# A planned kernel's first stores of weight sums and its transposing transfers: new dependences, new planned costs, a new order

## The chip, the cores and the metric

The kernel runs on one core of one Trainium2 chip. The metric is the device time of one execution in microseconds (us). The time before is 708.41 us, the median of 3 runs (707.8 to 711.64).

## The reference, cut to what matters

```python
xn = layernorm(x)                                  # x: 2048 x 1024, bf16
# A: sliding dilated attention, 32 heads of 32, 8 keys per query at distances 0, 2, ..., 14
q, k, v = split(xn @ wqkv)                         # wqkv: 1024 x 3072
attn = softmax(mask(q . k[pos - 2 w]) * 32 ** -0.5)
s = (sum_w attn[w] * v[pos - 2 w]) @ wo            # wo: 1024 x 1024
# B: gated product
g = silu((silu(xn @ w1) * (xn @ w3)) @ w2)         # w1, w3: 1024 x 3584, w2: 3584 x 1024
out = x + s * g
```

## The kernel before

The 2048 rows are four chunks (c) of 512 rows, two chunks to a block (b). A block goes through the q, k and v products, the gate and up products (14 steps of two 128-column tiles, numbered by f tile), the down product and the output product with wo; the attention of a chunk runs on VectorE (DVE) beside the products. Nearly every product of a block is done as a fast matrix product of the Strassen-Winograd kind: 2 by 2 parts (two chunks by two halves of the contraction), seven products in place of eight, with sums of the weights (S, in fp16, four per weight matrix, two to a 1 MB row buffer) and sums of the transposed rows (xs). In block 0 the weight sums are made on DVE and stored in DRAM by GpSimd (POOL) for block 1 to load.

**The start.** The rows of chunk 0 and chunk 1 (x0, x1) are loaded and normalized by tiles of 128 rows. Chunk 0 is transposed on TensorE (PE) by way of PSUM. Of chunk 1, row tiles 0 to 2 are transposed by six transposing transfers on SyncE (SP), one for each tile and half of the columns: turn1_0_0, turn1_0_1, turn1_1_0, turn1_2_0, turn1_1_1, turn1_2_1 (chunk, tile, half; made in turn_half, line 680 of the profile); tile 3 is transposed on PE (tp1_3, two halves). While they run, PE does the products of chunk 0 with the first and second half of the q and k weights (fq0 to fq3, fk0 to fk3). DVE then makes, in an order that is written out by hand (plan.chains): the weight sums qs0f, qs1f; the row sums xs0, xs0b; qs3f; xs1, xs2; qs2f; xs3. The sum qs3f overwrites the row buffer of x1, which the transfers read. qs0f and qs1f lie in the row buffer S[0], qs3f and qs2f in S[1]; qkv_sums stores each with one 1 MB store on POOL (put_sq0_0, put_sq0_1). After the chain come, in the planner's order, the sums of the k weights and the two additions of the first pair of q products, qc12 and qc22; the products that follow on PE write the banks that qc22 reads. SP goes on, behind the transposing transfers, with loads of w2 parts (w2q), whose sums DVE makes in gaps.

**What sets the order.** Nothing is issued in the order in which the program text stands. Each operation is an entry of a Plan: its engine, a name, a function that emits the instruction, lists of the cells that it reads and writes, its planned time on the engine (occ), and for a transfer its bytes. Plan.depend makes planned dependences from the lists; Plan.limits works due times back from the TensorE order; Plan.simulate walks through it with these costs and takes, on each engine, the ready entry with the earliest due time (ties by the place in the program):

```python
for i in sorted((i for i in ready[e] if ops[i].ready <= T), key=lambda i: (ops[i].limit, i)):
```

A transfer is planned to occupy one shared pipe for its bytes over its rate, and to land 1.3 us later. Plan.replay repeats the walk once for each entry of ORDER: an entry's first part adds to the due times of operations, given by their number in the plan, and its second part moves a TensorE operation from one place in TensorE's order to another. The order of the last walk is what is emitted, engine by engine. The instruction itself is made by the entry's function, as in the helper for transfers, which does not hand on the lists:

```python
plan.op(eng, name, lambda: e.dma_start(out=o(), in_=a()), rd, wr, occ, 0.0, nbytes=kb * 1024, late=late)
```

The semaphores on the chip are set by the framework from the tiles that the emitted instructions name. Some lists hold cells that stand for no tile: the four transposing transfers of a later chunk (turn2, turn3, in ln_turn, line 688; turn2 on ScalarE's (ACT) queue, turn3 on SP's) read a cell "pr" that a product marks.

**Block 0's down product**, about 245 to 330 us: chunks 2 and 3 are loaded into row buffers, normalized on ACT (mean2, var2, mean3, var3 and so on), and transposed by turn2 and turn3; the halves of w2 and of its sums are loaded into row buffers that come free (rhs_load). One of these, number 1350 in the plan, is the first half of w2 for the products de0_0 to de0_3 (rhs_load("w", 1, 1)), and number 1351 is the second; 1343 to 1345 are turn3_1 to turn3_3.

Of the kernel before, what the change touches and what calls it, by code (L numbers as in the profile page):

```python
# [10 lines left out]
FP16 = mybir.dt.float16  # L11
# [3 lines left out]
PE, DVE, ACT, POOL, SP = range(5)  # L15
# [27 lines left out]
class Plan:  # L43
# [209 lines left out]
    def replay(self):  # L253

        pes = self.pes = [o.idx for o in self.ops if o.eng == PE]
        self.simulate()
        for late, swaps in [((), ())] * 2 + list(ORDER):
            for i, d in late:
# [15 lines left out]
            o.emit()  # L274


ORDER = (((), ((29, 26), (29, 26), (29, 26), (29, 26), )),
((), ((27, 26), (27, 26), )),
((), ((27, 26), (27, 26), )),
(((647, -0.7), ), ()),  # L280
(((684, 1.9), ), ()),
(((684, 1.8), ), ()),
((), ((243, 242), )),
(((1076, 0.5), (684, 1.1), ), ((244, 242), )),
(((684, 3.3), (684, 7.4), ), ((245, 243), )),
(((1004, 1.1), (1175, 3.5), (1077, 0.7), ), ()),
(((695, -0.4), ), ()),
(((1074, 3.8), (1074, 5.3), (1077, 1.4), ), ((248, 247), )),
(((1077, 0.3), ), ((251, 250), )),
(((695, -0.3), (718, -0.3), (1077, 0.7), (690, 0.6), ), ()),  # L290
((), ((27, 26), (27, 26), )),
(((1012, -0.8), ), ((370, 368), )),
(((1010, 0.4), (1010, 0.5), (1006, 0.4), ), ()),
(((1006, -0.2), (999, 0.3), ), ((371, 369), )),
(((1010, 1.6), ), ((370, 369), )),
(((1010, 0.9), (1010, 0.7), ), ((368, 370), (371, 370), )),
((), ((371, 370), )),
(((1012, 1.5), ), ()),
(((1225, 0.3), (1217, 1.6), (1112, 9.6), ), ()),
(((1222, 0.9), (1223, -0.4), ), ()),  # L300
(((1192, 1), (1177, 0.7), (1180, 1.6), (1179, -1), ), ()),
(((1193, 10.9), (1193, 10.3), ), ()),
((), ((375, 377), )),
(((1012, 0.6), ), ((370, 369), )),
(((1220, -0.3), ), ()),
(((1175, 10.8), (1006, 0.2), (1175, 3.6), ), ((368, 371), )),
(((1276, 0.4), ), ()),
(((1126, 7.6), ), ((405, 403), )),
(((1305, 4.1), (1350, -4.2), (1311, 3.1), (1277, 4.6), (1174, 0.3), ), ((423, 417), )),
(((1347, 1.8), ), ((422, 417), )),  # L310
(((1174, 0.4), (997, 8.3), (1344, 1), (1304, 0.4), ), ()),
((), ((427, 426), )),
(((1347, 1.4), ), ()),
((), ((419, 417), )),
(((1174, 0.8), ), ()),
(((1176, 0.6), (1012, -0.6), ), ()),
(((1173, 0.3), (1004, 2), (1173, 0.4), (1174, 0.5), ), ()),
(((1012, -0.4), (1012, -0.2), (1012, -0.5), (1173, 0.8), ), ()),
(((1175, 0.5), ), ((377, 376), )),
(((1012, -0.4), (1012, -0.2), ), ((369, 368), )),  # L320
(((1472, 6.6), (1345, 0.5), (1343, 0.3), ), ()),
(((1387, -0.6), (1343, 0.3), ), ((435, 434), )),
((), ((27, 26), (27, 26), )),
((), ((25, 26), (25, 26), )),
((), ((458, 455), )),
((), ((456, 455), (456, 455), )),
((), ((458, 456), )),
(((1513, 0.2), ), ()),
(((1513, 0.7), (1513, 0.5), ), ()),
(((1527, 0.5), (1525, 0.6), ), ((461, 460), )),  # L330
(((2454, 7.2), (2448, 1.4), (2262, 1.3), (2067, -1.6), (2452, 3.5), (2262, 2.7), (2326, 2.7), ), ((756, 761), (761, 758), )),
(((2060, 0.7), (2066, 3.4), (2067, -3), (2061, 3.1), ), ()),
(((2326, -4), ), ()),
(((2069, -2.2), (2065, 1.6), (2452, 4), (2281, 2.7), ), ((761, 759), (457, 455), )),
(((1946, -0.3), (2326, -0.4), (2011, 2.5), (2026, 4.2), ), ()),
(((2312, 0.5), (2312, 0.4), ), ()),
((), ((457, 455), (455, 453), (457, 455), )),
(((1729, 4.5), (1679, 1.1), (2323, 0.9), ), ((594, 592), )),
(((2326, -0.3), (2334, 0.5), ), ()),
(((2312, 0.8), (1875, 0.4), ), ()),  # L340
((), ((593, 596), (598, 596), )),
(((1755, 0.5), (1752, 11.9), (1743, 15.3), (1878, -0.3), (1862, 0.6), (1748, 4.1), ), ((597, 595), )),
(((2310, 0.5), (2312, 0.3), ), ((761, 760), )),
)
LAST = []

# [2 lines left out]
def kernel(  # L349
# [13 lines left out]
    S, D, F = 2048, 1024, 3584  # L363
# [38 lines left out]
    sq_dram = {t: dram.tile([2, P, 4096], FP16, name=f"sq{t}_dram") for t in RL}  # L402
# [24 lines left out]
    plan = Plan()  # L427
# [84 lines left out]
    def dma(eng, name, o, a, rd, wr, kb, late=0.0):  # L512
        e = {SP: nc.sync, POOL: nc.gpsimd, ACT: nc.scalar}[eng]
        occ = {SP: 0.45, POOL: 0.58, ACT: 0.42}[eng]
        for part, cost in COST:
            if name.startswith(part):
                kb = kb * cost
                break
        plan.op(eng, name, lambda: e.dma_start(out=o(), in_=a()), rd, wr, occ, 0.0, nbytes=kb * 1024, late=late)
# [22 lines left out]
    def r8v(s, dt=BF16):  # L542
        a = s.ap()
        return a.bitcast(dt) if dt != BF16 else a
# [20 lines left out]
    def xrow(xt, st):  # L565
        return xt.ap().rearrange("p (s d) -> p s d", s=NST)[:, st, :]
# [110 lines left out]
    def turn_half(c, st, xt, kh):  # L677

        half, cut = c % 2, slice(kh * CH, (kh + 1) * CH)
        plan.op(SP, f"turn{c}_{st}_{kh}", lambda: nc.sync.dma_start(  # L680
            out=xT[:, half, kh * KH:(kh + 1) * KH, st * P:(st + 1) * P], in_=xrow(xt, st)[:, cut], transpose=True),
            [(xt, st)], xt_cells(half, kh, st), 0.7, 0.0, nbytes=128 * 1024)

    def ln_turn(c, st, xt, cell):

# [1279 lines left out]
```

## Time and profile before

| | |
|---|---|
| median of 3 runs | 708.41 us (707.8 to 711.64) |
| the profiled execution | 709.42 us |
| its span, first to last instruction | 707.6 us |
| granted TensorE clock | 1.0 |
| TensorE busy | 699.7 us, 99% |
| VectorE busy | 674.8 us, 95% |
| ScalarE busy | 399.0 us, 56% |
| HBM read and written | 161 MB, 228 GB/s over the span |

Columns of the timeline: start and length in us, engine, line, operation, written and read tiles, shape, count, and in brackets the engine's idle time just before with what ended it. Engines with a q are their sequencers; a transfer's issue is there, its landing is not. Lines are those of helpers: 478 is a product, 487 an addition, subtraction or multiplication on DVE, 492 a copy on ACT, 519 a plain transfer, 680 and 688 transposing ones. Tiles have the program's names without numbers: r is a row buffer, so r<-r,r on DVE is a sum of weights; xT the transposed rows; mm a PSUM bank; k a buffer of f32 halves; qo the q values. TENSOR_TENSOR r<-r,r and qo<-mm,k of about 1.2 us start 1.14 us apart when nothing holds them. The chain of waits has start, length and what was on it; the waits have total, times and longest.

### The profile page before, as it was taken

How to read it: one execution, taken by the hardware profiler on the slowest of the kernel's cores; microseconds unless marked ns; L12 is line 12 of the kernel's file. 1: busy time of each engine (PE TensorE's matmuls, PEld its weight loads, DVE VectorE, ACT ScalarE, POOL GpSimd, SP SyncE). 2: the span in 40 equal slices, each digit the busy share in tenths (PEclk: the TensorE clock that was granted, in tenths of full speed). 3: DMA queues.
4: the chain of work that ended last, by engine and by line, in shares of the span. 5: the costliest groups of instructions: out<-in, count | busy, mean ns of one | idle time of the engine just before them, and what ended most of it. 6: DMA issues, size and time to landing. Idle time of an engine off the chain costs nothing.

```text
span 707.6 us, 9945 instructions
## 1 busy us (share of the span) xinstructions
PE 699.7 (99%) x3666; PEld 374.1 (53%) x3666; DVE 674.8 (95%) x827; ACT 399.0 (56%) x752; POOL 48.4 (7%) x93
## 2 busy tenths in 40 slices
PE   8999999999999999999999999999999999999997
PEld 5555555555555474744555554555555555656443
DVE  7898999999999999999979999999999999999956
ACT  7644465758575799612555355656766865222233
POOL 1010011112110010100010000000100010000000
PEclk9999999999999999999999999999999999999999
DMA  9999898964986679894896559973766575957502
GB/s 324 289 413 383 266 340 309 324 221 138 355 282 213 233 249 253 283 272 124 333 323 245 178 175 337 315 234 131 223 219 198 188 220 173 349 189 242 178 27 92
DMA packets 138239, 174.06 MB, mean 246 GB/s; under 512 B 16912, under 2 KB 112800, under 8 KB 131536
## 3 DMA queue, kind: packets, MB, share of 16 engines
q1 hardware_dynamic: 126128, 132.33, 58.6%
q0 software_dynamic: 7408, 39.61, 15.0%
q10 hardware_dynamic: 4656, 1.51, 1.1%
q8 instruction: 28, 0.46, 0.3%
q14 instruction: 19, 0.16, 0.1%
HBM read 117.31 MB, written 43.78 MB: 228 GB/s over the span
## 4 chain that ended last, share of the span: by engine, by line
PE 83%; DVE 9%; DMA 3%; issue 2%; ACT 1%; SPq 1%; DVEq 0%; POOL 0%; ACTq 0%
PE mm L478 73%; PE mm L1423 6%; PE mm L1152 4%; DVE r L487 2%; DVE a L487 2%; DMA s_dram<-r 1%; DVE qo L487 1%; DVE h_sb L487 1%; DMA r<-in_A_wqkv_dram 1%; DVE k L487 1%; DMA r<-in_A_x_dram 1%; DMA xT<-r 0%; DVE mm L487 0%; DVE small L583 0%; ACT k L492 0%
## 5 line engine op out<-in xcount | busy, mean ns | idle before, releaser
L478 PEld LDWEIGHTS <-r 128*128 128x128 f16 (+1 forms) x2068 | 219.4, 108 | 200.8 <-issue 1.9
L478 PE MATMUL mm<-xs,r 128*128 128x512 f16 x1280 | 300.1, 379 | 1.3 <-DVE qo L487 0.8
L478 PE MATMUL mm<-xT,r 128*128 128x512 bf16 (+2 forms) x788 | 178.8, 370 | 1.7 <-DMA r<-in_A_wqkv_dram 1.0
L492 ACT COPY k<-mm 128x512 f32<-128x512 f32 (+1 forms) x226 | 123.6, 558 | 75.9 <-PE mm L478 69.3
L478 PE MATMUL mm<-r,h_sb 128*128 128x512 f16 (+1 forms) x592 | 129.7, 379 | 0.0
L492 ACT COPY mm<-mm 128x512 f32<-128x512 f32 (+1 forms) x157 | 76.4, 489 | 93.6 <-PE mm L1152 33.0
L478 PEld LDWEIGHTS <-h_sb 128*128 128x128 f16 (+1 forms) x680 | 66.5, 98 | 78.8
L487 DVE TENSOR_TENSOR a<-a 128x2048 bf16<-128x2048 bf16 (+7 forms) x106 | 107.1, 1011 | 0.7
L487 DVE TENSOR_TENSOR h_sb<-mm,k 128x1024 bf16<-128x1024 f32 x48 | 58.1, 1217 | 7.0 <-PE mm L478 7.0
L487 DVE TENSOR_TENSOR a<-qo,kT 128x2048 bf16<-128x2048 bf16 x48 | 57.7, 1217 | 0.2
L1152 PE MATMUL mm<-xT,r 128*128 128x256 f16 (+1 forms) x364 | 56.9, 273 | 0.0
L487 DVE TENSOR_TENSOR h_sb<-h_sb 128x1024 f16<-128x1024 bf16 (+7 forms) x74 | 54.3, 746 | 0.0
L487 DVE TENSOR_TENSOR a<-E,vT 128x2048 bf16<-128x2048 bf16 x42 | 50.2, 1216 | 0.0
L1152 PEld LDWEIGHTS <-r 128*128 128x128 f16 (+1 forms) x364 | 35.6, 98 | 26.5
L487 DVE TENSOR_TENSOR r<-r,r 128x1024 f16<-128x1024 f16 (+7 forms) x56 | 42.8, 768 | 3.0 <-DMA xT<-r 1.5
L509 ACT ACTIVATE k<-k 128x512 bf16<-128x512 f32 x56 | 32.2, 622 | 22.9 <-DVE k L487 22.9
L487 DVE TENSOR_TENSOR k<-mm,k 128x1024 f32<-128x1024 f32 (+1 forms) x44 | 44.9, 1022 | 0.2
L509 ACT ACTIVATE h_sb<-mm 128x512 bf16<-128x512 f32 x60 | 36.3, 606 | 13.6 <-PE mm L478 12.3
L487 DVE TENSOR_TENSOR qo<-qo,a 128x2048 bf16<-128x2048 bf16 x32 | 38.9, 1216 | 0.0
L487 DVE TENSOR_TENSOR r<-r 128x1024 f16<-128x1024 bf16 (+4 forms) x71 | 35.9, 514 | 0.8 <-DMA r<-in_A_wqkv_dram 0.8
L487 DVE TENSOR_TENSOR h_sb<-h_sb,k 128x2048 bf16<-128x2048 bf16 x28 | 34.0, 1216 | 0.0
L492 ACT CAST k<-mm 128x512 bf16<-128x512 f32 x56 | 31.4, 605 | 0.5 <-PE mm L478 0.5
(131 smaller groups left out, 535.9 us busy)
## 6 DMA issues: line engine op xcount, KB each, us to landing
r<-in_B_w_dram SPq DMA_DIRECT2D x42, 512.0 KB, 6.2
s_dram<-r POOLq DMA_DIRECT2D x14, 1024.0 KB, 6.1
r<-s_dram SPq DMA_DIRECT2D x14, 1024.0 KB, 5.0
r<-t_dram SPq DMA_DIRECT2D x15, 896.0 KB, 7.3
r<-in_A_wqkv_dram SPq DMA_DIRECT2D x10, 1024.0 KB, 7.4
r<-in_B_w_dram SPq DMA_DIRECT2D x11, 896.0 KB, 5.8
h_sb<-in_B_w_dram SPq DMA_DIRECT2D x14, 512.0 KB, 8.6
t_dram<-h_sb POOLq DMA_DIRECT2D x7, 1024.0 KB, 7.8
```

What stands on the lines that cost most here:

```text
L478: nc.tensor.matmul(cut(ps.ap()), lhsT=lhs[k](), rhs=cut(rhs[k]()), start=(first and k == 0), stop=(last and k == n - 1), skip_group_check= ...
L487: plan.op(DVE, name, lambda: fn(out=o(), in0=a(), in1=b()), rd, wr, occ, 0.08, late=late)
L492: plan.op(ACT, name, lambda: nc.scalar.copy(out=o(), in_=a()), rd, wr, occ, 0.11)
L509: plan.op(ACT, name, lambda: nc.scalar.activation(out=o(), in_=a(), func=ACTF.Silu), rd, wr, occ, 0.11, table="silu")
L1152: nc.tensor.matmul(half(pa[i].ap, n)(), lhsT=A[0][k](), rhs=B[0][k](), start=first and k == 0, stop=k == 1, skip_group_check=True)
L1423: nc.tensor.matmul(half(bank.ap, n)(), lhsT=a[k](), rhs=c[k](), start=first and k == 0, stop=k == NQ - 1, skip_group_check=True)
```

## The change

Three things are done. First, in block 0 the two stores of the q weights' sums (t = 0, the only call with early > 0) list as read, besides their own cells, those that turn1_1_1 and turn1_2_1 write. Second, the planned costs are new: a transposing transfer of chunk 1 is planned as 1.35 us of SP in place of 0.7 and as 1.4 times its bytes, the general rate of transfers is 3.45e5 bytes per us in place of 3.25e5, and 3.7e5 is set between the chunk-1 transfers and the weight sums of q. Third, ORDER is replaced: 118 entries in place of 67.

```diff
-ORDER = (((), ((29, 26), (29, 26), (29, 26), (29, 26), )),
+ORDER = (((), ((39, 44), (44, 42), )),
+((), ((39, 44), (44, 42), )),
+((), ((27, 26), )),
...
-(((1305, 4.1), (1350, -4.2), (1311, 3.1), (1277, 4.6), (1174, 0.3), ), ((423, 417), )),
-(((1347, 1.8), ), ((422, 417), )),
-(((1174, 0.4), (997, 8.3), (1344, 1), (1304, 0.4), ), ()),
...
-(((1472, 6.6), (1345, 0.5), (1343, 0.3), ), ()),
-(((1387, -0.6), (1343, 0.3), ), ((435, 434), )),
...
+(((1065, 0.5), ), ((222, 228), (228, 226), )),
...
+(((1175, 0.4), ), ((368, 364), )),
...
+((), ((454, 452), (457, 456), (452, 451), )),
...
+(((2060, 2.6), (2448, 5.9), (2058, 2.7), (2323, 0.7), ), ((539, 538), )),
...
@@ turn_half
-            [(xt, st)], xt_cells(half, kh, st), 0.7, 0.0, nbytes=128 * 1024)
+            [(xt, st)], xt_cells(half, kh, st), 1.35, 0.0, nbytes=int(1.4 * 128 * 1024))
@@ qkv_sums
-                dma(POOL, f"put_sq{t}_{i}", lambda i=i: sq_dram[t][i], lambda i=i: r8v(S[i], FP16), c(2 * i) + c(2 * i + 1), [("sqd", t, i)], 1024)
+                dma(POOL, f"put_sq{t}_{i}", lambda i=i: sq_dram[t][i], lambda i=i: r8v(S[i], FP16),
+                    c(2 * i) + c(2 * i + 1) + (xt_cells(1, 1, 1) + xt_cells(1, 1, 2) if early else []), [("sqd", t, i)], 1024)
@@ the program's loop over the blocks
-    RATE = 3.25e5
+    RATE = 3.45e5
...
-            plan.rate = RATE
+            plan.rate = 3.7e5
             qkv_first("k", wk, lambda j: ln_tp(1, j, x1, (ACT, ACT)), turned=3)
             xn_sums()
+            plan.rate = RATE
             sq = qkv_sums(b, 0, wq, 30.0, ([("ln", 1, 3)], [], xs_cells(1)))
```

Carried out one after the other, the exchanges of the old ORDER and of the new one give these TensorE orders where they differ: at places 39 to 43 the old has tp1_3, fk0, fk1, fk2, fk3 and the new fk1, tp1_3, fk0, fk3, fk2; at 417 to 424 the old has the halves of de0 in the order 0a, 2a, 3a, 0b, 1a, 1b, 2b, 3b and the new 0a, 0b, 1a, 1b, 2a, 2b, 3a, 3b; and the new moves single products at 222 to 232, 364 to 376, 451 to 462, 538 to 543, 823, 829 and 854, and no longer moves those at 426, 434, 592 to 598 and 756 to 761.

More of the change, by code (lines that the diff above doesn't have):

```diff
@@ L274, in run @@
             o.emit()
-ORDER = (((), ((29, 26), (29, 26), (29, 26), (29, 26), )),
+ORDER = (((), ((39, 44), (44, 42), )),
+((), ((39, 44), (44, 42), )),
+((), ((27, 26), )),
+((), ((27, 26), )),
 ((), ((27, 26), (27, 26), )),
-((), ((27, 26), (27, 26), )),
[L280 to L287, printed above, removed]
@@ L288 @@
-(((1074, 3.8), (1074, 5.3), (1077, 1.4), ), ((248, 247), )),
-(((1077, 0.3), ), ((251, 250), )),
-(((695, -0.3), (718, -0.3), (1077, 0.7), (690, 0.6), ), ()),
-((), ((27, 26), (27, 26), )),
[L292 to L308, printed above, removed]
-(((1305, 4.1), (1350, -4.2), (1311, 3.1), (1277, 4.6), (1174, 0.3), ), ((423, 417), )),
-(((1347, 1.8), ), ((422, 417), )),
-(((1174, 0.4), (997, 8.3), (1344, 1), (1304, 0.4), ), ()),
@@ L312 @@
[L312 to L320, printed above, removed]
-(((1472, 6.6), (1345, 0.5), (1343, 0.3), ), ()),
-(((1387, -0.6), (1343, 0.3), ), ((435, 434), )),
-((), ((27, 26), (27, 26), )),
-((), ((25, 26), (25, 26), )),
@@ L325 @@
[L325 to L343, printed above, removed]
+((), ((27, 26), )),
+((), ((24, 26), (24, 26), (24, 26), )),
+((), ((27, 26), )),
+((), ((44, 42), (42, 44), )),
@@ new lines @@
+((), ((27, 26), )),
+((), ((29, 26), (29, 26), (29, 26), )),
+((), ((29, 26), )),
+((), ((27, 26), )),
+((), ((25, 26), (25, 26), )),
+((), ((25, 26), (25, 26), )),
+((), ((27, 26), )),
+((), ((27, 26), )),
+((), ((45, 44), (45, 44), )),
+((), ((27, 26), )),
+((), ((27, 26), )),
+((), ((27, 26), )),
+((), ((27, 26), (27, 26), )),
+((), ((27, 26), )),
+((), ((40, 44), (44, 41), )),
+((), ((45, 44), (45, 44), )),
+((), ((44, 42), (44, 42), (43, 44), )),
+(((1065, 0.5), ), ((222, 228), (228, 226), )),
@@ new lines @@
+(((1067, 1), (1066, 2.4), (646, 2.3), (1066, 2), (653, 3.8), (1067, 1.8), ), ((222, 227), )),
+((), ((225, 226), (226, 223), )),
+((), ((229, 228), )),
+((), ((232, 230), )),
+((), ((231, 230), )),
+((), ((45, 44), (45, 44), )),
+((), ((226, 229), )),
+(((646, -0.5), ), ()),
+(((657, 12.1), (654, 4.5), (647, 0.8), (657, 10), ), ((229, 228), )),
+((), ((44, 43), (44, 43), )),
+((), ((44, 41), (41, 44), )),
+((), ((43, 44), (44, 41), )),
+((), ((44, 42), (42, 44), )),
+(((1175, 0.4), ), ((368, 364), )),
@@ new lines @@
+((), ((27, 26), (27, 26), )),
+(((997, 0.3), ), ()),
+(((1173, 0.9), ), ()),
+(((997, 0.3), (1173, 5.1), ), ((376, 372), )),
+((), ((371, 372), )),
+((), ((376, 371), )),
+((), ((43, 44), (44, 42), )),
+((), ((372, 371), )),
+((), ((370, 371), (370, 371), )),
+((), ((372, 371), )),
+(((1222, 0.2), (1220, -0.4), (1225, 0.7), ), ((373, 371), )),
+(((1177, 0.5), ), ()),
+(((1192, 4.3), ), ()),
+(((1177, 1), (1193, 12.1), (1193, 13.4), (1179, 0.9), ), ()),
+(((1173, 3.9), (1179, 1.1), ), ()),
+(((1177, 0.8), ), ()),
@@ new lines @@
+(((1220, -0.7), ), ()),
+(((1177, 8.8), ), ((374, 377), (377, 372), )),
+(((1173, 11.8), (1223, -0.4), ), ()),
+(((1222, 0.6), ), ()),
+(((1126, 3.6), (1312, -2.7), ), ()),
+(((1202, 0.7), ), ()),
+(((1179, 5.8), (1202, 12.6), (1179, 2.2), (1194, 0.3), ), ()),
+(((1277, 0.9), (1299, -0.5), ), ((405, 403), )),
+(((1180, 0.3), ), ()),
+((), ((458, 455), (455, 452), )),
+(((1433, -0.5), ), ()),
+(((1161, 0.5), ), ()),
+((), ((454, 452), (457, 456), (452, 451), )),
+((), ((462, 459), )),
+(((1179, 0.3), (1195, 0.4), (1220, -0.2), ), ((458, 456), )),
@@ new lines @@
+(((1180, 0.1), (1180, 0.5), ), ()),
+(((1513, 0.6), ), ()),
+(((1513, 4.2), ), ()),
+(((1528, 0.5), ), ()),
+((), ((461, 460), )),
+(((1180, 0.2), ), ()),
+(((1220, -0.2), ), ()),
+(((1179, 0.4), ), ()),
+(((1220, -0.1), ), ()),
+(((1179, 0.4), (1180, 0.2), ), ()),
+(((1179, 0.2), ), ()),
+(((1179, 0.3), ), ()),
+(((1220, -0.2), ), ()),
+(((1180, 3.1), (1180, 5.7), (1228, 0.5), ), ()),
+(((1241, -0.8), (1180, -1.1), (1180, -1.3), ), ()),
+(((1228, 1), (1227, 1.4), (1220, 1.7), ), ()),
+(((1299, 1.4), (1299, 1.9), (1194, 4.7), (1305, 1.1), (1304, -1.1), (1194, 3.9), (1221, 1), (1304, -1.3), (1277, 1.4), (1183, 0.3), ), ((374, 377), )),
@@ new lines @@
+(((1256, -0.2), (1236, 0.7), ), ((377, 376), )),
+(((2365, 0.2), (1179, 0.2), ), ()),
+(((2458, 0.4), (2463, 0.5), ), ()),
+(((1173, 4), ), ((826, 824), )),
+(((1119, 0.5), (2498, 9.9), (1181, 0.4), ), ()),
+(((2507, -1), (1225, 12.4), ), ()),
+(((2480, 0.5), (2532, 0.4), ), ((824, 823), )),
+(((1239, 0.8), ), ((823, 828), )),
+(((1180, 0.2), (1256, -1.6), (1195, 0.2), (1181, 1.1), ), ()),
+(((2060, 2.6), (2448, 5.9), (2058, 2.7), (2323, 0.7), ), ((539, 538), )),
+(((2290, -0.2), ), ((827, 826), (543, 538), )),
@@ new lines @@
+(((2470, 0.7), ), ()),
+(((1180, 0.5), (1195, 0.3), (1195, 0.4), ), ()),
+(((2511, -0.6), (1220, -0.2), ), ((822, 826), )),
+(((2509, 0.7), ), ()),
+(((1220, -0.3), (1180, 0.5), ), ((823, 822), )),
+((), ((827, 825), )),
+(((1180, 0.6), (1220, -0.2), (1180, 0.5), (2516, 0.7), ), ()),
+(((2511, 1.1), (2511, 0.8), (1179, 0.3), (2476, 1.3), ), ()),
+(((2511, -0.6), (2525, 0.5), ), ((825, 824), )),
+(((2476, 1), (2507, -1.6), ), ()),
+(((1179, 0.3), (2498, 1.6), (2476, 0.4), ), ((830, 828), )),
+(((2476, 6.7), ), ((825, 824), )),
@@ L344 @@
+(((2511, -0.3), (1180, 0.7), (2498, 2.5), (1180, 0.2), ), ()),
+(((1180, 0.5), (2475, 3), ), ((855, 854), )),
+((), ((827, 825), (825, 822), )),
+(((1195, 1.9), (2692, 4.4), (2591, 0.4), (2589, 0.9), ), ()),
+(((2695, 3.6), ), ()),
+(((1195, 0.2), ), ((829, 826), )),
 )
```

## The prediction

> **What bounds the kernel now.** I read the page first, for who is busy; then TensorE's waits, for what is left to win; then the timeline of the first 38 us, where most of it lies; then the chain of waits through it.
>
> ```profile
> PE 699.7 (99%) x3666; PEld 374.1 (53%) x3666; DVE 674.8 (95%) x827; ACT 399.0 (56%) x752; POOL 48.4 (7%) x93
> ```
>
> TensorE (PE) is the bound, and the change alters none of its matmuls. So the most that an order can win is PE's idle time. TensorE's waits, all of them over the whole span:
>
> ```profile
> PE mm L460 <- DVE k L458: 1.3, 1, 1.3
> PE mm L478 <- DMA r<-in_A_wqkv_dram: 1.0, 2, 0.6
> PE mm L478 <- DVE qo L487: 0.8, 1, 0.8
> PE mm L478 <- DVE r L487: 0.7, 1, 0.7
> PE mm L478 <- ACT k L492: 0.5, 1, 0.5
> ```
>
> The first two lie before 10 us, in what the change does not touch. The other three are 2.0 us. The timeline shows two of them behind the transposing transfers:
>
> ```profile
> 22.93 0.58 POOL L519 DMA_DIRECT2D sq_dram<-r  x1 [18.44 <-DMA xT<-r]
> ...
> 24.72 1.89 PE L478 MATMUL mm<-xs,r 128*128 128x512 f16 x8
> ...
> 26.02 1.23 DVE L487 TENSOR_TENSOR r<-r,r 128x2048 f16<-128x2048 bf16 x1 [1.49 <-DMA xT<-r]
> ...
> 27.30 1.92 PE L478 MATMUL mm<-xT,r 128*128 128x512 bf16 x8 [0.69 <-DVE r L487]
> ...
> 29.06 5.34 PE L478 MATMUL mm<-xs,r 128*128 128x512 f16 x24
> ...
> 30.94 0.55 POOL L519 DMA_DIRECT2D sq_dram<-r  x1 [7.43 <-DVE r L487]
> ...
> 31.70 1.22 DVE L487 TENSOR_TENSOR r<-r,r 128x2048 f16<-128x2048 bf16 x1
> 32.84 2.35 DVE L487 TENSOR_TENSOR qo<-mm,k 128x1024 bf16<-128x1024 f32 x2
> ...
> 35.23 1.89 PE L478 MATMUL mm<-xs,r 128*128 128x512 f16 x8 [0.84 <-DVE qo L487]
> ```
>
> One 512-column matmul takes (5.34 - 0.38) / 23 = 0.216 us, start to start (0.38 is the last one's own length). Eight from 24.72 free PE at 26.45; it starts at 27.30: stall one, 0.85 us. Twenty-four from 29.06 free it at 34.24; it starts at 35.23: stall two, 0.99 us. The same count gives 0.66 us for the third, at 249.1 us, where an ACT copy of a half product came late. Everywhere else PE starts a matmul when the one before allows it.
>
> Why stall one: the chain of waits names the last transposing transfer, turn1_2_1.
>
> ```profile
> 21.13 1.26 SPq L680
> ...
> 22.44 3.46 DMA xT<-r
> ```
>
> It is issued at 22.44, the issue takes SP 1.26 us as the one before did, and it lands at 25.89. The DVE sum qs3f, which overwrites the row buffer that this transfer reads, starts at 26.02 and ends at 27.24.
>
> **The change, part by part.** *The wait of the stores.* The first store of sums (put_sq0_0, POOL, 22.93) gets two more cells in its list of reads. I take this as costing and winning nothing on the chip, because that list goes only into the planner's dependences; the instruction emitted is a dma_start of S into DRAM, which names no part of xT. The trace of before has the same case. The transposing transfers of x2 have a "pr" cell in their list, which makes the plan hold each until the matmuls of its row tile are done. Here is the fourth of them in ACT's timeline, and below it PE's matmuls by shape from 272.4 to 275.6:
>
> ```profile
> 272.64 1.25 ACTq L688 DMA_TRANSPOSE xT<-r  x1
> ```
>
> ```profile
> L478 PE MATMUL mm<-r,h_sb 128*128 128x512 bf16 x15 | 3.4, 379 | 0.0
> ```
>
> The 14 matmuls whose cell it reads run from 272.43 to 275.62; the transfer went out 3.0 us before their end. Such a cell moves an instruction in its engine's queue and does not hold it there. In POOL's queue nothing stands before the store that it could be moved behind: its follower comes at 30.94, 8 us later. The row's "<-DMA xT<-r" does not speak against this: the store went out 0.29 us after its second sum (qs1f, done 22.64), and its follower 0.29 us after its own (30.65 to 30.94); that a first-half transfer landed at 22.68 is a coincidence of two of its semaphores. So turn1_2_1 still lands near 25.9, and stall one stays. The price if the store is held after all is the second rival.
>
> *Planning the transfers as 1.35 us of SP and 1.4 times the bytes.* No instruction changes. 1.26 us is what the trace shows for the last two, so the plan's xs and S sums now come later, as on the chip. This is what I expect to pay. In the trace xs3 ended at 31.78; then DVE took the first of the k sums (31.70, 1.22 us), then qc12 and qc22 (together 32.84 to 35.18), and qc22 released PE at 35.23. Yet the last input of qc12, an ACT copy, was there at 31.57. The k sum was put first by a plan that had xs3 done before that copy. The k sum and qc12 have the same due time (the first k product), and the planner breaks ties by the place in the program, where qc12 is earlier; once xs3 is planned late, qc12 is ready and goes first. Then qc12 runs 31.7 to 32.9, and qc22, whose last matmul ends at 32.67, from 33.0 to 34.2; PE, free at 34.24, goes on. Gain 0.98 us, bounds 0 (order kept) and 0.99. The k sum comes 2.3 us later; its reader starts at 42.14 and the sum was done at 32.92, so 6.9 us of cover remain. Closer is the first v sum, done at 58.61 after a weight load that landed at 57.4, for a product at 61.13: 2.5 us, of which a PE that is 1.0 us earlier eats 1.0; without that cover, each us late is a us of PE.
>
> *Swaps on PE.* Read off the exchanges: the second half of fk1 now stands between the two transposes of x1's last tile. Its weights landed at 21.16 and PE would reach it at 20.95: 0.21 us idle, hidden in stall one (PE waits for 27.24 anyway); 0.21 us if stall one goes. The other exchanges (the steps of tiles 10 to 13, the passage to the down product, the first q pairs of block 1, wo of chunk 1) move matmuls by one to six places in stretches where PE never waits; bounds -0.66 (the third stall goes) and +0.66 (another like it); I take 0.
>
> *Rates.* 3.45e5 for 3.25e5 bytes per us makes the plan expect 1 MB in 3.04 us and not 3.23. The 3.7e5 is set where no transfer is planned and does nothing. A load whose landing decides can come 0.2 us late for each MB before it; the tightest is the w2 load that landed at 298.16 for a product at 298.24. I take 0, keep +0.4.
>
> **The sum.** The profiled execution took 709.42 us: span 707.6 and 1.82 around it. 709.42 - 0.98 = 708.44. It lay 1.01 above the median of 708.41, so the median comes to 707.43, **707.4 us**.
>
> **Rivals.** (a) *The store is held.* Then turn1_2_1 has the DMA engines alone. turn1_1_1, which had, landed 1.35 us after its issue ended (22.39 to 23.74); turn1_2_1 took 2.19 (23.70 to 25.89). So it lands at 25.05, qs3f ends at 26.4, stall one goes and stall two with it: 707.4 - 0.85 = 706.6, up to 0.2 less gain by fk1. For it: the timeline's releaser, and that the store's first packets run at 24.25, in the transfer's last. Against: the paragraph above. The Trainium skill (DMA: Bandwidth & Descriptors, Anatomy of one DMA) gives a transfer some 2.0 us of fixed cost, most of it the receipt of the last write; counted from the end of the issue, an estimate from that page has it land at 25.7 and win only 0.2, so 707.2. It speaks against the change; the 1.35 us of turn1_1_1 does not bear it out. (b) *DVE's order stays.* qc22 still ends at 35.18, stall two stays: 708.4. (c) *Slower: a load behind a transposing transfer on SP, at 290 us.* These were the times of the x3 transfers' issues on SP:
>
> ```profile
> L688 SPq DMA_TRANSPOSE xT<-r x4: 1877/3460/6702, 291.2 to 304.4; - x4
> ```
>
> The old order pulls the deciding w2 load (number 1350 in the plan) 4.2 us forward, pushes those transfers back, and spreads the product's halves on PE; the new order drops all three. In the trace the load goes out at 289.40, ahead of turn3_0 at 291.25, with 0.08 us to spare at its reader. The plan books 2.3 us for such an issue, the trace 1.9 to 6.7. If the load falls behind one, PE waits for all of it: 707.4 + 1.9 to 6.7 = 709.3 to 714.1. It decides as soon as the load leaves SP over 0.1 us later. Against: the load's buffer is free at 289.3 and the transfers wait for products at 292 to 293 in the plan, which leaves it first in most orders.
>
> **How the numbers follow.** Forecast 0.53; (a) 0.10; (b) 0.17; (c) or a like load elsewhere 0.20. The forecast's own bounds are 706.8 to 708.5. The range goes from (a) with the third stall gone too, 706.6 - 0.66 = 705.9, less a tenth for its scatter, to 711.2, where the smaller part of (c) ends; the rest of (c) is left out. 0.5% is 3.5 us, about what a measurement of this kernel can tell from no change. Faster by that needs more than all three stalls (2.5 us): 0.02. Slower by that is the larger part of (c), above 711.95: 0.14. Within: 0.84.
>
> **What would show it.** Right: put_sq0_0 again near 22.9; turn1_2_1 landing near 25.9; PE's wait for DVE r still some 0.7; no wait for DVE qo, qc12 ahead of the k sum on DVE. Rival (a): the store after 25 and turn1_2_1 landing near 25.1. Wrong: new waits of PE of 1 us and more after 38 us, a DMA named at 298, or the wait for DVE qo still there.

## The result, and the profile after

The changed kernel takes 714.09 us (median of 22 runs, 711.27 to 716.19), the kernel before 708.67 beside it (22 runs, 706.96 to 713.23). The ratio is 1.0059, 95% interval [1.0043, 1.0074]: 0.6% slower. The forecast was 707.4.

Executions whose mean granted TensorE clock is a little lower tend to be longer, so I also give medians without them: 12 executions of the changed kernel had a clock of 0.999 or 1.0, with a median of 712.3 us, and 10 had 0.997 or 0.998, with 714.6 (a low clock, below). Single times of the two groups overlap. In all comparisons below together the kernel before had a low clock in 27 of 117 executions. Beside the first kernels its other executions had a median of 708.6 and the low ones 711.6.

The profiled execution took 714.69 us, its span is 712.9 (before: 709.42 and 707.6). The page and TensorE's waits over the whole span:

```profile
PE 698.8 (98%) x3612; PEld 374.3 (53%) x3666; DVE 675.1 (95%) x827; ACT 398.2 (56%) x752; POOL 48.2 (7%) x93
```

```profile
PE mm L529 <- DVE r L538: 2.7, 1, 2.7
PE mm L529 <- DVE h_sb L538: 2.0, 2, 1.8
PE mm L529 <- DMA r<-in_A_wqkv_dram: 1.4, 3, 0.5
PE mm L511 <- DVE k L509: 1.3, 1, 1.3
PE mm L529 <- DMA r<-in_B_w_dram: 0.2, 1, 0.2
```

(Lines are 51 higher than before; 54 matmul records are missing in this trace, so offsets below go by the weight loads, PEld, which are complete.) The waits for DVE qo and for ACT k are gone. The wait for DVE r has grown from 0.7 to 2.7, and a wait for DVE h_sb is new. The timeline of the head and the chain of waits through it:

```profile
22.62 0.58 POOL L570 DMA_DIRECT2D sq_dram<-r  x1 [18.13 <-DMA xT<-r]
...
25.13 1.89 PE L529 MATMUL mm<-xs,r 128*128 128x512 f16 x8
...
28.47 1.23 DVE L538 TENSOR_TENSOR r<-r,r 128x2048 f16<-128x2048 bf16 x1 [3.77 <-DMA xT<-r]
...
29.76 3.37 PE L529 MATMUL mm<-xT,r 128*128 128x512 bf16 x8 [2.74 <-DVE r L538]
```

```profile
22.62 5.74 DMA xT<-r
```

The store still goes out at 22.62; it is not held. But turn1_2_1, issued in the same moment, lands 5.74 us later, at 28.35, where before it took 3.46. TensorE's wait costs more than its length. Stretches of the span, with the busy times of PE, PEld, DVE, ACT and POOL and at the end the granted clock, the DMA share and GB/s:

```profile
24.00:28.00 4.00, 2.96 (x13) 1.48 (x12) 0.71 (x2) 2.99 (x6) 0.00 (x0) 1.00 1.00 287
28.00:32.00 4.00, 2.24 (x6) 0.88 (x7) 3.53 (x4) 0.65 (x2) 0.00 (x0) 0.67 0.99 358
32.00:36.00 4.00, 4.00 (x19) 1.90 (x18) 3.71 (x4) 1.17 (x2) 0.55 (x1) 0.91 1.05 393
```

Behind the wait the first six matmuls start 0.43 us apart, not 0.216. The second new loss lies at 387 us. The chain of waits before it:

```profile
360.20 5.46 DMA out_dram<-r
...
365.78 0.38 SPq L570
...
368.32 8.10 DMA E<-a
...
388.39 1.15 DVE h_sb L538
389.54 0.04 issue
389.58 5.56 PE mm L529 x25
```

The 1 MB load wqkv1_1 of pass 2 leaves SP at 365.78, once a store (out_dram<-r, 360.20) has landed, and the four returns of the softmax weights, E1, leave right behind it. The last of these, issued at 368.32, lands at 376.42. VectorE's softmax steps (a<-E,vT) start there, and the k weights' quantities (h_sb<-mm,k), queued behind them, reach TensorE at 389.54, after a wait of 1.79 us. SP's queue has the load ahead of the returns before the change too; there it leaves 4.2 us earlier, and the E1 have landed by 370.6. SP before, then after:

```profile
361.54 0.39 SPq L519 DMA_DIRECT2D r<-in_A_wqkv_dram  x1
362.63 3.63 SPq L519 DMA_DIRECT2D E<-a  x4
```

```profile
365.78 0.38 SPq L570 DMA_DIRECT2D r<-in_A_wqkv_dram  x1
366.26 2.73 SPq L570 DMA_DIRECT2D E<-a  x4
```

TensorE's offset against the kernel before, by the weight loads, gives the ledger:

| where | us |
|---|---|
| 21.4: fk1 first, waits for wqkv1_1 | +0.40 |
| stall one, 0.69 to 2.74 | +2.05 |
| half rate behind it | +1.29 |
| stall two gone | -0.84 |
| 170 | +0.32 |
| third stall (249) gone | -0.71 |
| 259 to 310, the most of it at 298 to 301 | +0.51 |
| 387, E1 | +1.95 |
| rest | +0.32 |
| sum | +5.29 (span: +5.3) |

The first two rows are one loss of 2.46 us: the landing of turn1_2_1 sets TensorE's restart, at 29.76 in place of 27.30, whether or not it has stood 0.40 at 21.4 first. The third stall is gone in the profiles of kernels with the whole old order too (before_hold and before_e1, below); only the profile of before has it. So its row says nothing of the change.

### The profile page after: what moved, and what is told of

Same layout as the page of the kernel before. It is cut to its first block, busy times and chain, and to the rows that moved or that the text cites. A ratio compares the mean times of both kernels' runs of the same rounds, so it can differ in the third digit from the quotient of the medians.

```text
span 712.9 us, 9902 instructions
## 1 busy us (share of the span) xinstructions
PE 698.8 (98%) x3612; PEld 374.3 (53%) x3666; DVE 675.1 (95%) x827; ACT 398.2 (56%) x752; POOL 48.2 (7%) x93
## 4 chain that ended last, share of the span: by engine, by line
PE 75%; DVE 11%; DMA 6%; issue 6%; SPq 1%; ACT 0%; DVEq 0%; POOLq 0%
PE mm L529 67%; PE mm L1204 5%; DVE a L538 4%; PE mm L1475 3%; DMA r<-in_B_w_dram 2%; DVE r L538 2%; DVE qo L538 1%; DVE h_sb L538 1%; DMA E<-a 1%; DMA r<-in_A_wqkv_dram 1%; DMA xT<-r 1%; DMA out_dram<-r 1%; DVE xs L538 1%; DVE k L538 1%; SPq L570 1%
## 5 line engine op out<-in xcount | busy, mean ns | idle before, releaser
L529 PE MATMUL mm<-xT,r 128*128 128x512 bf16 (+2 forms) x749 | 175.0, 372 | 6.2 <-DVE r L538 2.7
```

Of the source, the lines that this page charges most:

```text
L529: nc.tensor.matmul(cut(ps.ap()), lhsT=lhs[k](), rhs=cut(rhs[k]()), start=(first and k == 0), stop=(last and k == n - 1), skip_group_check= ...
```

## The experiments

Operations go by their number in the plan; "a behind b" puts a right behind b in the order that is emitted.

**1. Is it the store against the transfer?** Three kernels. In two the store is really held: a copy of two elements that turn1_1_1 and turn1_2_1 write is put ahead of it on POOL. In the third the first store of the old kernel is cut in two, and its first half starts before the transfer. A fourth moves wqkv1_1.

```diff
+# after_hold, before_hold: ahead of put_sq0_0
+nc.gpsimd.tensor_copy(out=hold_t[:], in_=xT[:, 1, KH, 2 * P - 1:2 * P + 1])
+# before_two: put_sq0_0 as two stores of half the columns, the first behind qs0f
+# after_e1: 1524 (wqkv1_1) behind 1470 (the last E1)
```

> The changed kernel, with a two-element GpSimd copy out of the cells of turn1_1_1 and turn1_2_1 put ahead of the first store, so that the store really waits for them. Theory 1 (the first store reaches the DMA engines together with the last transposing transfer, and that transfer then lands behind it): the store goes out at 24.5 to 26, turn1_2_1 lands 2.4 to 2.8 us after its issue begins (28.35 - 22.62 = 5.7 in the changed kernel's profile), TensorE's wait for DVE r falls from 2.7 to under 0.5, the time falls by 2 to 3 us, to some 711 to 712. Rival (the new order of the copies and products at the start is what makes stall one longer): the store is late, the wait stays at 2 us or more, the time stays at 714.

> The kernel before with the same copy ahead of its first store, its order unchanged. Theory 1: turn1_2_1 lands near 25.1, stall one (0.7 in the waits, 0.85 by the matmuls) goes, stall two stays or shrinks, 0.5 to 1.0 us less than the kernel before in its faster executions, some 707.3, and the executions at 711 to 713 us, if they are those in which the store came first, become rare. Rival (the copy or the later store costs more than the stall, because the store's 1 MB is then moved while the w2 loads want the engines): the wait goes and another comes, time the same or up to 2 us more.

> The kernel before with its first store cut in two: the first half (512 KB) goes out as soon as qs0f is done, about 1.3 us earlier, the second as before. Theory 1: the first half is now always ahead of the last transposing transfer, which lands at 27 to 28.5 in place of 25.9; stall one is 1.8 to 3 us; the time is 1 to 3 us above the faster executions of the kernel before, and all executions are like that. Rival (the landing of 25.9 is set by SP's issue and the transfer's own length): it lands at 25.5 to 26.2 and the time is the same.

> The changed kernel with the second half of block 1's k weights (wqkv1_1, 1 MB) issued on SP behind the four transfers of chunk 1's softmax weights (E1) and not in front of them. Theory 3 (the E1 transfers on SP land behind that load, and DVE's values, and with them qc22 of the k products, are late): E1 on SP lands 5 to 7 us after its issue and not 9, DVE's wait for it (1.0 in the page) goes, TensorE's wait for DVE h_sb of 1.8 near 387 us goes or falls under 0.5, the time falls by 1.5 to 2 us, to some 712.5. Rival (the E1 transfers are slow because the engines are full with the stores and loads of that stretch, whatever goes first on SP): E1 still lands 8 us and more after its issue, and the load, now behind, is waited for: same or slower by up to 2 us.

Measured: after_hold 713.78 us (5 executions), ratio to before 1.0079 [1.0049, 1.011]; before_hold 709.21, 1.0001 [0.9986, 1.0016]; before_two 711.62, 1.0043 [1.0024, 1.0061]; after_e1 710.93, 1.0017 [0.9995, 1.004]. What the profiles say of the transfer turn1_2_1:

| kernel | transfer issued | store issued | landed | took |
|---|---|---|---|---|
| after_hold | 21.96 | 25.78 | 24.44 | 2.48 |
| before_hold | 22.76 | 26.57 | 25.24 | 2.48 |
| before | 22.44 | 22.93 | 25.89 | 3.46 |
| after_e1 | 21.93 | 22.58 | 25.19 | 3.26 |
| after | 22.62 | 22.62 | 28.35 | 5.74 |
| head_after (below) | 22.57 | 22.48 | 28.08 | 5.52 |
| before_two | 22.04 | 21.53 | 28.79 | 6.75 |
| before_two_fill (below) | 21.99 | 21.19 | 29.55 | 7.56 |

So it is a race. About half a microsecond of lead costs the transfer 0.8 to 1.1 us against the held store; a tie, or the store first, costs it 3 to 5 us. All profiles here fall this way. In all four profiles of the old head with its own store the transfer won. Whether the old order loses the race in some of its executions, the 23% with a low clock among them, is not shown: before_hold, where it can't be lost, had no low clock in 10 executions and before_two had 8 in 10, but before_late below, where it can't be lost either, had 5 in 10, and head_after, which lost it in its profile, had none in 10. Nor is it shown why the changed kernel had 10 low clocks in 22 and after_e1 and head_after, with the same head, none in 19 together.

But holding the store did not pay. before_hold stayed level, and after_hold no better than the change itself. TensorE got through stall one 2 us early and stood later. VectorE in after_hold, then in after_e1, where the race was won:

```profile
48.71 1.90 DVE L539 TENSOR_TENSOR h_sb<-h_sb 128x1024 f16<-128x1024 bf16 x3 [2.55 <-DMA h_sb<-in_B_w_dram]
50.53 2.35 DVE L539 TENSOR_TENSOR h_sb<-mm,k 128x1024 bf16<-128x1024 f32 x2
```

```profile
59.89 1.23 DVE L542 TENSOR_TENSOR r<-r,r 128x2048 f16<-128x2048 bf16 x1 [4.23 <-DMA r<-in_A_wqkv_dram]
```

In after_hold VectorE has a w2 sum (175) ahead of the k weights' quantities, and waited 2.55 us for its load: a TensorE wait of 2.37 at 52.9. In after_e1 it has the v sum qs0 (285) first of four, and waited 4.23 us for its load wqkv2_1, which landed at 59.79: two TensorE waits, 1.26 and 1.48. With the load wqkv1_1 behind them the E1 returns took 4.8 to 5.5 us, and the wait of 1.8 us at 387 was gone. That the move cures this wait is shown. What made the load leave late in the changed kernel is not: before_hold, in the old order, had the same wait (1.25 us at 384.9), and after_hold, in the new order, only 0.45 at 388.

**2. VectorE's order, or the transfers?**

```diff
+# after_hold_dve: after_hold, and 175 behind 264, 176 behind 175, 285 behind 284
+# after_hold_dve_e1: and 1524 behind 1470
+# before_hold_ks_e1: before_hold, and 237 (first k sum) behind 216 (qc22), 1524 behind 1470
```

> The changed kernel with the store of the q weights' first sum truly held (as in after_hold, 713.8 us) and three steps of VectorE put later, nothing else: the w2 sums 175 and 176 behind the k weights' quantities qc12 and qc22 (261, 264), and the v weights' sum qs0 (285), which needs the late load wqkv2_1, behind qs2, qc12 and qc22 (288, 281, 284). Theory (the new order gives back what the hold gains, because VectorE waits at 46 to 49 and at 57 to 65 us for loads that land 2.5 to 4 us after their planned time, with the quantities that TensorE needs queued behind): the PE stall of 2.37 us at 52.9 goes, none over 0.7 us comes up to 70 us, and the time falls by about 2.4 to 711.4. Rival (the loads themselves are the bound of that stretch, whatever VectorE does first): TensorE waits there all the same, 713 to 714.

> As after_hold_dve, and the load wqkv1_1 of pass 2 (op 1524) behind the four returns of the softmax weights E1 (1463, 1465, 1468, 1470) on SP. If the losses of the head and of the 387 us stretch are separate terms they add: 711.4 less 1.8 to 3 (after_e1 stood 3.2 below the changed kernel) is 708.4 to 709.6, level with the kernel before. If the second only takes back time that the first would have cost anyway (TensorE bounded later by the transfers of pass 2), nothing more is gained: 711.

> The kernel before with three single steps: the store truly held until both last transposing transfers are in, the k weights' sum qs0 (237) behind qc12 and qc22 (213, 216) on VectorE, and wqkv1_1 of pass 2 behind the E1 returns on SP. Theory: what the change aimed at is worth its stalls when it is done without the new order: before_hold (709.2) had PE stalls of 0.74 at 34.6 and 1.25 at 384.9; without them 707.2, and no execution at 711 to 713. Rival (other work takes the place of each removed stall): 709.

Measured: 716.53 us, 1.0112 [1.0095, 1.013] (4 executions, all at a low clock); 715.91, 1.0098 [1.0079, 1.0118] (4, all at a low clock); 709.07, 0.9994 [0.9975, 1.0014]. My theory of VectorE's order fell. after_hold_dve lost the wait at 52.9 and got one of 3.67 at 62.8, and a long stretch at half rate:

```profile
52.00:60.00 8.00, 7.08 (x33) 3.76 (x31) 7.50 (x8) 2.59 (x5) 1.06 (x2) 1.00 1.02 418
60.00:64.00 4.00, 1.20 (x3) 0.44 (x4) 2.45 (x2) 0.00 (x0) 0.00 (x0) 0.65 1.07 356
64.00:68.00 4.00, 4.00 (x11) 1.51 (x10) 1.23 (x2) 1.66 (x3) 1.06 (x2) 0.50 1.10 388
```

```profile
61.52 3.74 DVE L543 TENSOR_TENSOR r<-r,r 128x2048 f16<-128x2048 bf16 x3 [2.02 <-DMA r<-in_A_wqkv_dram]
```

The columns ahead of the clock are the busy times of PE, PEld, DVE, ACT and POOL. The DMA share is 1.0 or more at 418 GB/s, and wqkv2_1, issued at 42.79, lands at 61.49. Whatever VectorE does first, the v sum of that load can't start before. In before_hold_ks_e1, 1.9 us ahead at 35 us, VectorE was the one without room, busy but for 0.78 us from 31 to 47:

```profile
PE mm L483 <- DVE qo L492: 1.5, 1, 1.5
...
```

**3. Fewer transfers ahead of the one that decides.**

```diff
+# after_late: after_hold, 1524 behind 1470, on SP the w2 loads 173, 174 behind 250 (wqkv2_1);
+#   on DVE 285 behind 284, the w2 sums 175..178 behind 286, 287, 1022, 1023; their store 179 behind 290
+# before_late: before_hold_ks_e1, 173 behind 250, sums 161..164 behind 233, store 165 behind 242
```

> The changed kernel with the store truly held, wqkv1_1 of pass 2 behind the E1 returns, and the two w2 loads 173 and 174 (512 KB each) put behind wqkv2_0 and wqkv2_1 on SP, the w2 sums 175 to 178 behind the v weights' sums as in the order before, their store 179 behind the v sums' stores, and 285 behind 284. Theory (the stretch 24 to 60 us is full of transfers, 410 to 425 GB/s with the DMA share at 1.0; TensorE, freed of both early stalls, arrives 2 us early at 60 and waits there for wqkv2_1, 3.67 us in after_hold_dve, and runs at a granted clock of 0.50 after so long a stall): with 1 MB fewer ahead of it, wqkv2_1 lands 2.4 us earlier (1 MB at 420 GB/s), at 59 or before, the stall at 61 to 63 falls under 1.5 us, the clock stays at 1.00, and the time is 716.5 less 4 to 5: 711 to 712. Rival (the stall there is VectorE's order, not the transfers): 715 to 717 as after_hold_dve.

> before_hold_ks_e1 (709.1; its freed 1.9 us came back as a PE stall of 1.53 us at 43.7, where VectorE had waited 0.78 us for a w2 load and did w2 sums ahead of the quantity) with the w2 sums 161 to 164 behind the quantities qc22, qc12 (236, 233) on VectorE, their store 165 behind put_sq1_1, and the w2 load 173 behind wqkv2_1. Theory (each removed stall comes back only where a full VectorE or full transfers are next, and these moves clear both): no PE stall over 0.5 us between 26 and 70 us, 707.5. Rival (the stretch is bounded by VectorE or the transfers whatever the order): a new stall of 1 to 2 us at 45 to 65 and 709.

Measured: after_late 710.26 us, 1.0000 [0.9974, 1.0025], every execution at a clock of 1.0; before_late 710.03, 1.0006 [0.9982, 1.003]. In after_late wqkv2_1 lands at 56.22 in place of 61.49, and TensorE's wait there (DVE r) is 0.7:

```profile
...
PE mm L534 <- DMA r<-in_B_w_dram: 0.9, 1, 0.9
PE mm L534 <- DVE r L543: 0.7, 1, 0.7
...
```

The earlier landing shows that in this stretch the transfers are the bound. Against after_hold_dve_e1 (715.91) the moves of the w2 loads, their sums and their store are worth 5.7 us together, the half rate behind the long wait included; what the 1 MB of loads is worth alone was not measured. The head is then 1.0 us faster than that of before; the wait of 0.9 for a w2 load at 299.8 is among what is lost again later. before_late got the rival's outcome, somewhat larger: the freed time came back as a wait of 2.32 at 52.6, behind the w2 sums that I had moved there.

**4. Head or rest?** Both orders put the same 358 operations before 84 us; so they can be crossed.

```diff
+# head_before: these 358 in the order of before, the rest in the changed order; head_after: the reverse
+# head_before_e1: head_before, and 1524 behind 1470; before_e1: before, and 1524 behind 1470
+# best: the head of after_late, the rest of before, 1524 behind 1470
+# after_late_mid: after_late, 255 to 315 us in the order of before
```

> The changed kernel whose instructions up to about 84 us (358 planned steps that both orders put there) stand in the order of before; from there on the order of the change. Theory (two separate losses): the head costs what it does before, with stall one and two (2.9 us less than after at 147 us), and the rest what it does after (+0.3 at 173, -0.7 at 250, +0.4 at 301, +1.95 at 388, +0.3): 711.0. If the loss is the head's alone: 708.7. If the rest's alone: 714.

> The counterpart of head_before: instructions up to about 84 us in the changed order, the rest in the order of before. Theory (two separate losses): the head's loss alone, 2.9 us where the store meets the last transposing transfer and 1 to 2 where not, with before's gaps after that: 710 to 712. If the rest carries all the loss: 708.7.

> head_before (before's order up to 84 us, the changed order after it; 712.1 us in the executions at a mean granted clock of 0.999 or more, 716.1 in those below) with one step put back: the load wqkv1_1 of pass 2 behind the four returns E1 on SP. Theory (the loss behind 84 us is mostly the E1 returns landing 7 us later behind that load, with the k weights' quantities queued behind the softmax steps that wait for them): 709 to 710.5, and the executions at 715 to 719 go. Rival (the loss is spread over the moved products): 712 or more.

> The kernel before with only wqkv1_1 of pass 2 behind the E1 returns on SP. If the order of before loses there too (before_hold had a stall of 1.25 us at 384.9, the profiled execution of before none): 708.0 or less, with a narrower spread. If that stall came only with the held store: 708.7.

> The order of after_late up to about 84 us (store held, w2 loads 173 and 174 behind the v weights' loads), then the order of before, with wqkv1_1 of pass 2 behind the E1 returns. Theory (the two losses are separate, and the head's gain of 1.0 us in after_late and the third stall, gone in every run with another head, are real): 708.6 less 1.0 less 0.5 is 707.1, all executions at a clock of 0.999 or more. Rival (each freed us comes back at the next full resource): 708.6 to 709.5.

> after_late (710.3), with the instructions between about 255 and 315 us in the order of before, the rest as after_late. In after_late and in the changed kernel ScalarE does statistics of chunk 3 ahead of the variances of chunk 2, so the last transposing transfer of chunk 2 goes out 3.8 us later, meets two 1 MB loads and lands at 282 to 285 in place of 276; in after_late 2.2 us of TensorE are lost between 287 and 300. Theory (that stage is the second loss behind 84 us, beside the E1 returns): no PE stall over 0.3 us from 284 to 302, and 708.0 to 708.6, level with best. Rival (the loss sits at 98 to 111 and 170 us, or moves on): 709.5 or more.

| kernel | us | ratio to before | executions at clock 0.998 or less |
|---|---|---|---|
| head_before | 714.94 | 1.0073 [1.0046, 1.01] | 6 of 10 |
| head_after | 709.69 | 0.9994 [0.997, 1.0017] | 0 of 10 |
| head_before_e1 | 712.04 | 1.0054 [1.0025, 1.0083] | 3 of 10 |
| before_e1 | 710.96 | 1.0014 [0.9991, 1.0038] | 3 of 10 |
| best | 708.0 | 0.9981 [0.9963, 0.9998] | 0 of 12 |
| after_late_mid | 710.58 | 1.0012 [0.9994, 1.003] | 0 of 10 |

The rest carries more of the loss than the head, which I had not thought. Without low clocks the changed kernel stands 3.7 us above before, head_before 3.2 (712.1 to 708.9) and head_after 1.5 (709.7 to 708.1), though head_after lost the race in its profile (a wait of 2.5). Of head_before's median, putting the E1 returns first takes back 2.9 us, but their intervals overlap, and without the low clocks it is 712.1 to 711.7. In the changed kernel itself it was 714.09 to 710.93 (after_e1), and 712.3 to 710.9 without low clocks; there the intervals do not overlap. So its share lies between 0.4 and 3.2 us. before_e1 does not gain by it: the profile of before had no wait there. What is left of the rest's loss is not in one place, and its cause stays open: the profile of head_before_e1 has waits of 0.2 to 0.4 at 99, 112 and 172 and 0.5 for a w2 load at 300. after_late_mid was to show the stage of that load as its cause, and failed: with the stage in the old order the wait is there all the same, 1.1 us at 299.9. Why the load is late there stays open.

best stands below both kernels, if barely: its interval ends at 0.9998. Without low clocks it is level with before (708.0 to 708.1); what it gains is that none of its 12 executions had one, against 7 of 35 of before beside it. Its profile has one wait over 0.4 us behind 10 us, that of the full transfers:

```profile
...
PE mm L533 <- DVE r L542: 0.7, 1, 0.7
...
```

**5. Is the low clock a second price of the stall?** before_two with twelve matmuls by a tile of zeros, put into the wait.

```diff
+for k in range(12):   # ahead of the product that waits for qs3f (207)
+    nc.tensor.matmul(ps.ap(), lhsT=zero_t[:], rhs=xT[:, 0, 0, :], start=False, stop=False, skip_group_check=True)
```

> before_two (711.6; the first store is split and starts before the last transposing transfer, TensorE waits 3.7 us at 26.5 to 30.2) with 12 matmuls of 512 columns by a tile of zeros, added to the bank of the waiting product ahead of it: 2.6 us of TensorE inside the stall, the result unchanged. Theory (a stall of that length costs itself and, behind it, some microseconds at a granted clock of 0.5): the wait shrinks to about 1.2 us, the granted clock from 28 to 36 us is 1.00 in place of 0.76 and 0.81, and the time falls by 1.5 to 710, with no execution below a mean clock of 0.999. Rival (the low clock comes of something else, or only the arrival of the transfer counts): 711.6 and a clock below 1 as before.

Measured: 711.11 us, 1.0025 [1.0, 1.005]; low clocks in 2 of 10 in place of 8 of 10. The profiled execution was one of the two. TensorE's timeline and its stretches (PE, DVE and ACT busy on mm tiles, clock, DMA share, GB/s):

```profile
26.01 2.75 PE L482 MATMUL mm<-xT,zero_t 128*128 128x512 bf16 x12
30.95 3.19 PE L484 MATMUL mm<-xT,r 128*128 128x512 bf16 x8 [2.19 <-DVE r L493]
```

```profile
28.00:32.00 4.00, 1.81 (x8) 0.00 (x0) 0.00 (x0) 0.93 1.04 394
32.00:36.00 4.00, 4.00 (x14) 0.00 (x0) 0.55 (x1) 0.64 1.05 387
```

Filling the wait took the low clock out of most executions, which bears out that it hangs on the idle time. In this profile the transfer landed even later than in before_two (7.56 us after its issue), so the wait that was left is 2.19 us and not the 1.2 I expected, and that was still enough for the low clock. The gain in time, 0.5 us, is inside the noise, less than the 1.5 I expected.

## Why the prediction was wrong, point by point

*The store's extra cells hold nothing on the chip:* right. The store went out at 22.62, as its sums allowed; in after_hold, where it is really held, it goes out at 25.78.

*"So turn1_2_1 still lands near 25.9, and stall one stays":* the first step that failed. It landed at 28.35. I took a landing from one execution as a constant. It is the outcome of a race whose margin in that trace was 0.49 us (22.44 against 22.93), and I had the hint in my own text: the store's first packets ran in the transfer's last. The spread of the three runs that I was shown, 707.8 to 711.64, was wide, and I did not ask why; whether this race is in it is not shown. TensorE went on at 29.76 in place of 27.30: 2.46 us in the profile, and 1.29 of half rate behind it. On rival (a): really held, the transfer lands 1.2 us after its issue has ended, near the 1.35 that I took from turn1_1_1.

*What a stall costs.* Not in my sum at all: TensorE ran at half rate behind a stall. In after that is 1.29 us, in after_hold_dve some 2.6. The Trainium skill (TensorE: Matmul & The Clock Gate, The HAM clock gate) has the array fall to half its clock after an idle window of about 3.4 us that runs on its own phase, and rise again after as long a busy one. The half rate agrees (0.43 against 0.216 us from matmul to matmul), and so does the way back: the low spells in the clock records of these traces last 3.41 us, that of after_hold_dve 6.83. The length of the wait does not agree: waits of 2.32 (before_late) and 2.74 us (after) drew the half rate, of 2.37 (after_hold) and 2.52 (head_after) did not. That waits so alike end differently fits a window with a phase of its own, but no run shows the phase.

```profile
52.00:56.00 4.00, 3.40 (x9) 1.43 (x9) 3.41 (x4) 0.62 (x2) 0.53 (x1) 0.61 1.02 407
```

```profile
28.00:32.00 4.00, 2.52 (x12) 1.39 (x13) 3.80 (x4) 0.60 (x2) 0.00 (x0) 1.00 0.97 339
```

The first line is before_late, behind its 2.32; the second head_after, with its 2.52.

*Stall two goes, -0.98:* near in size (-0.84), but not by the mechanism that I gave, so the hit is luck. I had the quantity qc12 go ahead of the k sum (r<-r,r) on VectorE. It did not: the k sum still stands ahead of both quantities (qo<-mm,k) in after, and in every kernel with the new head.

```profile
34.16 1.22 DVE L538 TENSOR_TENSOR r<-r,r 128x2048 f16<-128x2048 bf16 x1
35.29 0.42 DVE L538 TENSOR_TENSOR xT<-xT 128x512 f16<-128x512 bf16 x1
36.68 2.35 DVE L538 TENSOR_TENSOR qo<-mm,k 128x1024 bf16<-128x1024 f32 x2 [0.97 <-PE mm L529]
```

What turned is the order of the two quantities: qc22, for which TensorE had waited, now comes first. after_e1, without the late landing, shows that this is enough: there the pair runs from 32.47 to 34.82, behind the k sum, and TensorE goes on at 33.5 without a wait. So the sign that I gave for "right", qc12 ahead of the k sum, did not come, and rival (b)'s condition, VectorE's old order, stayed for the k sum, and yet the stall went. That the gain stays was wrong too: I named the cover, the first v sum with 2.5 us, and judged it enough. It is the place where the freed time came back in after_e1 and after_hold_dve; in after_hold it came back earlier, at 52.9, behind a w2 sum. The new order has one more w2 load (174, planned at 35 us in place of 53) ahead of the v weights' loads, in a stretch where the DMA engines are full. I priced the new rate at +0.4 and did not look at which loads the new plan put early. Which part of the change moved that load no run shows: no kernel here takes the dependences, the planned costs and the order one at a time.

*fk1 first, 0.21, hidden:* hidden, as I said. TensorE stood 0.40 there and not 0.21, and would have stood that much longer at stall one without it.

*"The other exchanges: 0, bounds ±0.66":* the second step that failed, and the larger one in the medians. I took the order behind 84 us as nothing, and the orders crossed there put its loss at some 3.2 us of 3.7 (712.1 against 708.9 without low clocks). In the profile 1.95 of it stand where the E1 returns went out behind a load that left 4.2 us late; moving that load is worth 0.4 to 3.2 us, and where the remainder comes from stays open. The third stall did go (-0.71), but it is gone in kernels with the old order too.

*The rivals.* (a) and (b) did not come. (c), a load in front of small transfers on SP, was the right kind of mechanism at the wrong place: at 290 us the w2 load went first as I argued and cost TensorE only 0.15; at 366 a load stood ahead of small returns in both orders, and what differed was how long it waited there. With 0.20 it got too little: where an order of 2,800 operations is replaced, many such places are unseen. Of my signs for a wrong forecast, a new wait of over 1 us after 38 us, the one at 387 came. The time, 714.09, lies at the top of what I gave (c), and above my range.

## What to carry to other kernels

Price a stall by what comes next, and look for the resource that is full behind it: here the 2 us that TensorE won at 30 us were kept past 60 us only after two w2 loads, with their sums and their store, were moved out of the way. Treat a landing next to another transfer's start as a race, and ask by how much it was won. When an order is replaced, compare every queue of it, and at the head of each ask what it waits for: a w2 load had moved ahead of the v weights' loads, while the load that held the E1 returns up had not moved, it only left later. And look whether a stall that goes does so by the step that you gave for it.

## What the runs showed of the hardware

A transposing transfer of 128 KB landed 2.47 to 2.49 us after its issue began when a store of 0.5 or 1 MB from another queue was held back, 3.3 to 3.6 us after when the store started 0.4 to 0.7 us behind it, and 5.5 to 7.6 us after when the store started with it or up to 0.8 us ahead of it. TensorE fell to half rate behind waits of 2.2 to 4.9 us, for 2.6 to some 5 us, and not behind every one of that length (not behind 2.37 and 2.52). From 32 to 60 us the DMA engines moved 391 to 418 GB/s at a share of about 1.0 in the profiles where the transfer won or the store was held, and two 1 MB loads issued there between 40 and 45 us took 7.2 to 20 us to land.
